# Loading the last chunk of the wq weights as 112 rows and two times 8 rows, so that half of the DMA engines carry more of it

## Chip, cores, metric

One core of one Trainium2 chip. The metric is the device time of one execution in microseconds (us), lower is better; the span of a profiled execution is about 2 us shorter than its device time (138.2 against 140.57 us before the change).

## The reference, cut to what matters

A decode step of one transformer block for 4 sequences: layer norm, attention with 32 query heads over the last 2048 cached positions, then a gated feed-forward layer.

```python
# x [4,1,1024]; caches [4,4,8192,128]; wq [1024,4096]; wo [4096,1024]; w1,w3 [1024,3584]; w2 [3584,1024]
q = layernorm(x) @ wq                       # the first use of weights; wq is the first tensor loaded
p = softmax(q @ k^T * Dh**-0.5)             # k, v: the last 2048 positions
h = x + (p @ v) @ wo
out = h + (silu(ln(h) @ w1) * (ln(h) @ w3)) @ w2      # ln: layernorm
```

There are only 4 rows of activations, so nearly all the work is reading 55.6 MB of weights and cache once.

## The kernel before

Everything large goes through one ten-deep pool of tiles of 128 partitions x up to 16 KB in SBUF, the core's on-chip memory. The Sync engine issues the loads in a fixed order (wq, k, v, wo, w1, w3, w2), as far ahead as the pool allows. A wq chunk puts two neighbouring rows of the weights on each partition: one run of 16 KB of HBM per partition. "Rows" below are partitions of such a tile.

```python
stream = ctx.enter_context(tc.tile_pool(name="stream", bufs=10))
wq_v = A_wq.rearrange("(p kc) n -> p kc n", kc=KC)       # KC = 8, KPC = 2: four chunks

def load_wq(c):
    wq_t = stream.tile([P, KPC, Hq * Dh], BF16, tag="s")
    nc.sync.dma_start(out=wq_t[:], in_=wq_v[:, c * KPC : (c + 1) * KPC, :])
    return wq_t

plan = (
    [("wq", load_wq, (c,)) for c in range(KC // KPC)]
    + [("k", load_k, (b,)) for b in range(B)]
    # ... v, wo, w1, w3
    + [("w2", load_w2, (j, [4, 3] if j < JG - 1 else [3, 2, 1, 1])) for j in range(JG)]
)
# ... load_next(10) at the start; one more whenever a tile has been used
```

Of the kernel before, what the change touches and what calls it, by code (L numbers as in the profile page):

```python
# [10 lines left out]
P = 128  # L11
# [8 lines left out]
def kernel(  # L20
# [13 lines left out]
    nc = tc.nc  # L34
# [7 lines left out]
    KC = D // P  # L42
# [36 lines left out]
    KPC = 2  # L79
# [3 lines left out]
    wq_v = A_wq.rearrange("(p kc) n -> p kc n", kc=KC)  # L83
# [2 lines left out]

    def load_wq(c):
        wq_t = stream.tile([P, KPC, Hq * Dh], BF16, tag="s")
        nc.sync.dma_start(out=wq_t[:], in_=wq_v[:, c * KPC : (c + 1) * KPC, :])
        return wq_t  # L90

    def load_k(b):
# [33 lines left out]
    def load_w2(j, pieces):  # L126
# [6 lines left out]
# [4 lines that stand above are left out]
        + [("v", load_v, (b,)) for b in range(B)]  # L137
# [26 lines left out]
    for j in range(JG):  # L164
        nc.scalar.dma_start(
            out=x_q[QD * j : QD * j + B, :], in_=x_flat[:, j * CG : (j + 1) * CG]
# [7 lines left out]
    for c in range(2):  # L174
# [8 lines left out]
        out=xn[:], in0=x_sb[:], scalar1=mv[:, 0:1], scalar2=rstd[:, 0:1],  # L183
# [25 lines left out]
    for j in range(2, JG):  # L209
        nc.vector.tensor_tensor(  # L210
            out=same[:, 0, :], in0=same[:, 0, :], in1=ident[:, j * QD : (j + 1) * QD], op=ALU.add
# [6 lines left out]
    for kc in range(KC):  # L218
        wq_t = loaded["wq"][kc // KPC]
# [16 lines left out]
    for r in range(REP):  # L236
        nc.tensor.transpose(out=qt_ps[:, r, :], in_=q_sb[:, r * Dh : (r + 1) * Dh], identity=ident[:])
    nc.vector.tensor_copy(
        out=qz[:, :, : Hkv * QD].rearrange("p b (g z) -> p b g z", g=Hkv)[:, :, :, :REP],
        in_=qt_ps[:].rearrange("p r (g x) -> p x g r", g=Hkv)[:, :B, :, :],  # L240
# [24 lines left out]
    for u, (b, n) in enumerate(units):  # L265
        k_v = loaded["k"][b][:].rearrange("p (j d) -> p j d", d=Dh)
        kT = ktpool.tile([P, NJ, P], BF16, tag="kT")
        for t in range(NJ // TB):
            kt_ps = psA.tile([P, TB, P], BF16, tag=f"kt{nt % 4}")
            for jj in range(TB):  # L270
                nc.tensor.transpose(  # L271
                    out=kt_ps[:, jj, :], in_=k_v[:, n * NJ + t * TB + jj, :], identity=ident[:]
# [23 lines left out]
        out=Pm[:].rearrange("q (c jq) -> q jq c", jq=NSB), in_=scores_ps[:].rearrange("q (jq c) -> q jq c", jq=NSB),  # L296
# [42 lines left out]
    for hh in range(RPO):  # L339
        nc.vector.tensor_copy(  # L340
            out=o4[hh * MP : (hh + 1) * MP, :, :, :].rearrange("p h r b -> p r h b"),
            in_=o4_ps[hh * MP : (hh + 1) * MP, :, :, hh, :],
# [12 lines left out]
    for h4 in range(Hq // RPO):  # L355
# [35 lines left out]
        out=hn[:], in0=h1[:], scalar1=tot[:, 0:1], scalar2=rstd2[:, 0:1],  # L391
# [5 lines left out]
    for r in range(KPC):  # L397
# [3 lines left out]
        out=hnT[:], in_=hn_ps[:].rearrange("p r (j x) -> p j r x", j=JG)[:, :, :, :B]  # L401
# [34 lines left out]
    for i in range(IF):  # L436
# [3 lines left out]
        out=hgT[:], in_=hg_ps[:].rearrange("p i (j x) -> p i j x", j=JG)[:, :, :, :B]  # L440
# [52 lines left out]
```

## Time and profile before

| | before |
|---|---|
| time, median | 140.01 us (3 runs), 140.41 us over 6 runs |
| span of the profiled execution | 138.2 us |
| moved by DMA | 55.74 MB |
| PE (TensorE matmuls) busy | 54% of the span |

The DMA engines bound it. On the page, the two rows of the second part that matter are the mean busy share of the core's 16 DMA engines (in tenths, 40 slices of 3.5 us) and what they moved:

```profile
span 138.2 us, 2365 instructions
...
DMA  5999999999999999999999999999999999999950
GB/s 154 433 423 436 417 436 436 441 413 432 441 402 409 420 421 416 425 423 430 429 429 417 425 442 424 428 432 428 432 428 432 432 432 413 421 427 430 409 216 2
```

Between the first slice and the last two there is no dip: time is bytes over rate, and what lowers the rate anywhere is paid at the end. The chain of work that ended last says the same; its PE part runs beside a queue that stays full (DMA share 1.01 from 35 to 128 us).

```profile
DMA 74%; PE 16%; ACT 5%; SPq 1%; issue 1%; DVE 0%; ACTq 0%
```

The table by stretches (start:end, length, then busy us and instructions of PE, of PE's weight loads, of VectorE, ScalarE and GpSimd, then the granted clock, the DMA share and GB/s) gives the rate. The last wq chunk is loaded from about 17 to 22 us, then comes k:

```profile
12.00:17.00 5.00, 1.88 (x16) 0.51 (x16) 0.00 (x0) 0.00 (x0) 0.00 (x0) 1.00 0.99 423
17.00:23.00 6.00, 2.23 (x20) 0.61 (x23) 0.00 (x0) 0.00 (x0) 0.00 (x0) 1.00 1.01 434
23.00:29.00 6.00, 4.23 (x39) 2.46 (x32) 1.40 (x3) 0.60 (x1) 0.00 (x0) 1.00 1.02 437
29.00:35.00 6.00, 5.70 (x64) 4.07 (x63) 2.35 (x4) 3.79 (x4) 0.00 (x0) 1.00 1.00 426
```

And the same table shows the end, where the DMA share falls in steps because the engines do not end together:

```profile
130.00:132.00 2.00, 0.94 (x16) 0.45 (x19) 0.00 (x0) 0.00 (x0) 0.00 (x0) 0.50 1.00 408
132.00:133.00 1.00, 0.66 (x12) 0.26 (x5) 0.00 (x0) 0.00 (x0) 0.00 (x0) 0.50 0.72 283
133.00:134.00 1.00, 0.89 (x12) 0.32 (x12) 0.00 (x0) 0.00 (x0) 0.00 (x0) 0.50 0.43 164
```

The trace also has a record of every DMA packet (start, duration, size, queue). It does not name the engine, but an engine's next packet starts 3 to 4 ns before its last one ends, so its packets can be followed by their phase (what is said below of single engines is read in this way). Per engine a 128-row wq chunk is 8 packets of 16 KB at 0.611 us, one every 0.607 us. Eight packets of 16 KB belong to the queue that the page calls instruction (0.88 to 0.97 us each); they are called instruction fetches here after its name. After each of them one further engine lands every later DMA about 1.4 us behind; one 8 KB packet of another queue at 58.9 us costs one more engine 0.83 us. At the end seven engines are done at 132.2 to 132.5 us, one at 133.3 and eight at 133.6 to 133.9.

### The profile page before, as it was taken

The numbers are of one execution on the slowest core, as the hardware profiler recorded it, in microseconds if no ns is written. First come the engines' busy times: TensorE is split into PE (matmuls) and PEld (weight loads), VectorE is DVE, ScalarE is ACT, GpSimd is POOL, SyncE is SP. The second block draws the span as 40 slices with busy tenths as digits, with TensorE's granted clock in tenths as the row PEclk, the third lists the DMA queues.
The fourth block names the chain that finished last, engine by engine and source line by source line (L and its number), as shares of the span: only waits on it lengthen the run. The fifth ranks groups of instructions, "written<-read, shape, count | busy, mean of one in ns | idle before, by whom it ended". The sixth has DMA issues, their size and how long they took to land.

```text
span 138.2 us, 2365 instructions
## 1 busy us (share of the span) xinstructions
PE 75.0 (54%) x1057; PEld 43.4 (31%) x1057; DVE 37.1 (27%) x71; ACT 29.4 (21%) x29; POOL 0.7 (1%) x6
## 2 busy tenths in 40 slices
PE   0152254499798989300795489383244432663560
PEld 0111011295656556000795356131011110231220
DVE  6610000244343434520500460600008930300000
ACT  1200000126464646279420000000051000000000
POOL 2000000000000000000000000000000000000000
PEclk9999999999999999955555556855555555555555
DMA  5999999999999999999999999999999999999950
GB/s 154 433 423 436 417 436 436 441 413 432 441 402 409 420 421 416 425 423 430 429 429 417 425 442 424 428 432 428 432 428 432 432 432 413 421 427 430 409 216 2
DMA packets 7025, 55.74 MB, mean 403 GB/s; under 512 B 580, under 2 KB 612, under 8 KB 3560
## 3 DMA queue, kind: packets, MB, share of 16 engines
q1 hardware_dynamic: 6960, 55.58, 95.7%
q8 instruction: 8, 0.13, 0.3%
q10 hardware_dynamic: 56, 0.02, 0.1%
q14 instruction: 1, 0.01, 0.0%
HBM read 55.59 MB, written 0.01 MB: 402 GB/s over the span
## 4 chain that ended last, share of the span: by engine, by line
DMA 74%; PE 16%; ACT 5%; SPq 1%; issue 1%; DVE 0%; ACTq 0%
DMA w_t<-in_B_w_dram 55%; DMA k_t<-in_A_k_cache_dram 14%; PE kt_ps L271 10%; DMA wq_t<-in_A_wq_dram 5%; ACT kT L277 5%; PE scores_ps L256 5%; SPq L118 1%; PE y_ps L448 0%; DVE res L458 0%; ACT res L459 0%; SPq L111 0%; ACTq L277 0%
## 5 line engine op out<-in xcount | busy, mean ns | idle before, releaser
L277 ACT COPY kT<-kt_ps 128x1024 bf16<-128x1024 bf16 x16 | 15.9, 1013 | 14.5 <-PE kt_ps L271 14.5
L271 PE MATMUL kt_ps<-ident,k_t 128*128 128x128 bf16 x256 | 18.0, 231 | 0.9 <-DMA k_t<-in_A_k_cache_dram 0.9
L271 PEld LDWEIGHTS <-k_t 128*128 128x128 bf16 x256 | 15.9, 104 | 6.1 <-issue 4.9
L275 DVE COPY kT<-kt_ps 128x1024 bf16<-128x1024 bf16 x16 | 11.1, 692 | 17.6 <-PE kt_ps L271 17.6
L223 PE MATMUL q_ps<-wq_t,xnT 128*4 128x512 bf16 x64 | 7.5, 620 | 11.2 <-DMA wq_t<-in_A_wq_dram 11.2
L414 PE MATMUL u_ps<-w_t,hnT 128*4 128x448 bf16 x64 | 6.7, 567 | 10.3 <-DMA w_t<-in_B_w_dram 10.3
L256 PE MATMUL scores_ps<-kT,qz 128*32 128x512 bf16 x64 | 9.9, 609 | 3.0 <-ACT kT L277 3.0
L414 PEld LDWEIGHTS <-hnT 128*4 128x4 bf16 x128 | 3.9, 109 | 24.0 <-issue 23.4
L448 PE MATMUL y_ps<-w_t,hgT 128*4 128x256 bf16 x112 | 7.5, 404 | 6.3 <-DMA w_t<-in_B_w_dram 6.0
L414 PE MATMUL g_ps<-w_t,hnT 128*4 128x448 bf16 x64 | 6.5, 570 | 5.0 <-DMA w_t<-in_B_w_dram 4.7
L323 PE MATMUL OT_ps<-PT_sb,v_t 128*128 128x8 bf16 x256 | 7.4, 168 | 1.7 <-issue 1.4
L323 PEld LDWEIGHTS <-v_t 128*128 128x128 bf16 x256 | 7.3, 104 | 1.9 <-issue 1.7
L359 PE MATMUL y_ps<-wo_t,o_954 128*4 128x256 bf16 x128 | 6.4, 391 | 1.7 <-DVE y_ps L349 1.7
L223 PEld LDWEIGHTS <-xnT 128*4 128x4 bf16 x64 | 2.0, 106 | 15.8 <-issue 15.5
L309 PE MATMUL pt_ps<-Dm,Pm 128*128 128x128 bf16 x16 | 1.9, 308 | 9.3 <-DVE Dm L302 9.3
L459 ACT CAST res<-y_ps 128x128 bf16<-128x128 f32 x1 | 0.3, 267 | 31.0 <-DVE res L458 31.0
L448 PEld LDWEIGHTS <-hgT 128*4 128x4 bf16 x112 | 3.5, 103 | 10.3 <-issue 8.4
L427 DVE RECIPROCAL eg<-eg 128x896 f32<-128x896 f32 x1 | 5.8, 5753 | 0.0
L359 PEld LDWEIGHTS <-o_954 128*4 128x4 bf16 x128 | 4.0, 119 | 4.1 <-DVE y_ps L349 2.0
L233 DVE TENSOR_SCALAR q_sb<-q_ps 128x512 bf16<-128x512 f32 x1 | 0.7, 693 | 16.9 <-PE q_ps L223 16.9
L234 ACT ACTIVATE q_sb<-q_ps 128x512 bf16<-128x512 f32 x1 | 0.6, 597 | 20.9 <-DVE q_sb L233 20.9
L295 ACT ACTIVATE Pm<-scores_ps,nmax 128x2048 bf16<-128x2048 f32 x1 | 4.8, 4784 | 0.0
(73 smaller groups left out, 40.7 us busy)
## 6 DMA issues: line engine op xcount, KB each, us to landing
w_t<-in_B_w_dram SPq DMA_DIRECT2D x8, 1792.0 KB, 33.2
wq_t<-in_A_wq_dram SPq DMA_DIRECT2D x4, 2048.0 KB, 11.6
k_t<-in_A_k_cache_dram SPq DMA_DIRECT2D x4, 2048.0 KB
v_t<-in_A_v_cache_dram SPq DMA_DIRECT2D x4, 2048.0 KB, 40.4
wo_t<-in_A_wo_dram SPq DMA_DIRECT2D x4, 2048.0 KB
w_t<-in_B_w_dram SPq DMA_DIRECT2D x3, 1024.0 KB
w_t<-in_B_w_dram SPq DMA_DIRECT2D x4, 768.0 KB, 29.7
w_t<-in_B_w_dram SPq DMA_DIRECT2D x1, 512.0 KB
```

What stands on the lines that cost most here:

```text
L223: nc.tensor.matmul(q_ps[QD * g : QD * g + B, hf * 512 : (hf + 1) * 512], lhsT=xnT[:, kc, :], rhs=wq_t[:, kc % KPC, c0 : c0 + 512], start=( ...
L256: nc.tensor.matmul(scores_ps[QD * g : QD * (g + 1), n * 512 : (n + 1) * 512], lhsT=qz[:, b, g * QD : (g + 1) * QD], rhs=kT_v[:, g, :, :], ...
L271: nc.tensor.transpose(out=kt_ps[:, jj, :], in_=k_v[:, n * NJ + t * TB + jj, :], identity=ident[:])
L275: nc.vector.tensor_copy(out=kT[:, t * TB : (t + 1) * TB, :], in_=kt_ps[:])
L277: nc.scalar.copy(out=kT[:, t * TB : (t + 1) * TB, :], in_=kt_ps[:])
L295: nc.scalar.activation(out=Pm[:].rearrange("q (c jq) -> q jq c", jq=NSB), in_=scores_ps[:].rearrange("q (jq c) -> q jq c", jq=NSB), func=A ...
L309: nc.tensor.matmul(pt_ps[:, jj, :], lhsT=Pm[:, (jb * JPB + jj) * P : (jb * JPB + jj + 1) * P], rhs=Dm[:], start=True, stop=True)
L323: nc.tensor.matmul(OT_ps[:, b, g * REP : (g + 1) * REP], lhsT=v_t[:, g, j, :], rhs=PT_sb[:, j, g * QD + b * REP : g * QD + (b + 1) * REP], ...
L359: nc.tensor.matmul(y_ps[QD * j : QD * j + B, :], lhsT=o4[:, h4, r, :], rhs=wo_t[:, h4 % (HPC // RPO), r, j * CG : (j + 1) * CG], start=(h4 ...
L414: nc.tensor.matmul(out_ps[QD * j : QD * j + B, hf, :HF], lhsT=hnT[:, k2, r, :], rhs=w_t[:, r, c0 : c0 + HF], start=(k2 == 0 and r == 0), s ...
L427: nc.vector.reciprocal(out=eg[:], in_=eg[:])
L448: nc.tensor.matmul(y2_ps[QD * j : QD * j + B, :], lhsT=hgT[:, i, jf, :], rhs=w2_t[:, i, j * CG : (j + 1) * CG], start=False, stop=(jf == J ...
```

## The change

Its intent is to even out that end. The last wq chunk is cut into 112 rows, which all 16 engines load (7 rows each), and twice 8 rows, which only eight of them load. Those eight carry 9 packets of this chunk and the other eight carry 7. The trace of the changed kernel shows it: the 112-row DMA has 16 landings, and each of the sixteen engines has 7 packets of it; the two 8-row DMAs have 8 landings each; and when the next load, the first k tile, has landed, eight engines lie within 0.66 us of the first and eight 1.22 to 1.83 us behind it.

```diff
     def load_wq(c):
         wq_t = stream.tile([P, KPC, Hq * Dh], BF16, tag="s")
-        nc.sync.dma_start(out=wq_t[:], in_=wq_v[:, c * KPC : (c + 1) * KPC, :])
+
+        cuts = [0, P] if c < KC // KPC - 1 else [0, P - 16, P - 8, P]
+        for p0, p1 in zip(cuts[:-1], cuts[1:]):
+            nc.sync.dma_start(out=wq_t[p0:p1], in_=wq_v[p0:p1, c * KPC : (c + 1) * KPC, :])
         return wq_t
```

## The prediction

> **What bounds the kernel.** The DMA engines. The page gives a span of 138.2 us, 55.74 MB at 403 GB/s, a DMA share of 9 tenths or more in nearly every slice, PE 54% busy. In the chain of waits DMA has 74%; its last piece is the last of w2 (landed at 134.29 us), then about 0.8 us of matmuls and copies. The PE stretch in that chain (27.5 to 57 us) costs nothing: the queue stays full beside it, and a load issued at 58.4 us lands 33 us later.
>
> **The tail is uneven.** In the table by stretches the DMA share is 1.00 up to 132 us, then 0.72 and 0.43. The trace's packet records show why. Each engine moves one 16 KB wq row in 0.607 us, back to back. Eight 16 KB instruction fetches (0.88 to 0.97 us each) each put one further engine about 1.4 us behind for good; an 8 KB packet at 58.9 us puts another 0.83 us behind. So seven engines end at 132.2 to 132.5 us, one at 133.3, eight at 133.6 to 133.9. Followed by phase, the four engines that load x took none of the eight fetches; one of them took the 8 KB packet. [...] I infer that the late eight are the upper half.
>
> **What the change does.** [...] Lower half: 9 packets for the chunk instead of 8; upper half 7: +0.607 us and -0.607 us. SP issues two more DMAs (0.33 to 0.42 us each), early, under a full queue: nothing. The last wq chunk lands later: off the path.
>
> **Case A: rows cost what they cost now.** Upper half ends at 133.0 to 133.3, seven lower engines at about 133.1, but the one with the 8 KB packet at 133.3 + 0.6 = 133.9, where the end is today. Gain 0 to 0.1 us, at most 0.6: 139.4 to 140.2 us.
>
> **Case B: the destination is narrow.** Rows 112 to 119, then 120 to 127, are written by eight engines at once. [...] all of it on the critical path: 143 to 145 us. No run so far shows such a limit: every large load has 128 rows.
>
> I hold B slightly likelier (55%).
>
> **Predicted:** 142.0 us, 8 times in 10 within 139.6 to 145.2. Faster by over 2%: 0.01; within 2%: 0.46; slower: 0.53.
>
> **What would show it.** Packets of the two small DMAs: 0.61 us means A, 2 us or more B. The tail: in B a DMA share near 0.5 for 3 us or more; in A all engines end within about 1 us. wq's last chunk lands 0.6 us later in A, 4 or more in B.
>
> **What would make it wrong.** The late engines being the lower half (A then costs 0.6 us); the 112-row DMA colliding on ports too (worse than B); the semaphore rotation, shifted by two DMAs, draining the queue.

"Lower half" and "lower engines" are the eight engines that load the 8 rows, "upper half" the other eight; "port" is a way into SBUF that rows share, an assumption that no trace names. Case B came to 143 to 145 us, which is 3.6 to 4.8 us over the 139.4 to 140.2 of case A; it stands as the author's estimate.

## The result

| | before | after |
|---|---|---|
| time, median of 6 runs | 140.41 us | 146.96 us |
| ratio to before | 1 | 1.0474, 95% interval 1.0449 to 1.0499 |
| span of the profiled execution | 138.2 us | 144.9 us |

A ratio here is the mean time of one kernel's fast runs over the mean of the other's fast runs of the same rounds, so it is not quite the ratio of the medians. Executions over 1.5% slower than the fastest of the same kernel are left out of the means. The measured time lies above the predicted range (139.6 to 145.2). Which step of the prediction failed is told below.

The page after, the lines that answer to those of before:

```profile
span 144.9 us, 2368 instructions
...
DMA  5999999799999999999999999999999999999940
GB/s 156 426 435 434 425 280 213 100 407 434 425 430 417 399 420 421 421 417 427 430 425 430 423 425 437 424 439 427 427 424 427 439 431 413 425 424 426 413 187 2
...
DMA 74%; PE 15%; ACT 5%; SPq 2%; issue 1%; DVE 0%; ACTq 0%
```

Read the two rows together. For three slices the bytes moved fall to 280, 213 and 100 GB/s, while the share of busy DMA engines stays at 9 tenths or more in two of them. It reads 7 in the third, because a packet is counted whole in the slice in which it starts; the stretches below give 1.03 there. The engines are not idle; their packets take longer. All other slices before the end are much as before. The stretches:

```profile
12.00:17.00 5.00, 1.88 (x16) 0.51 (x16) 0.00 (x0) 0.00 (x0) 0.00 (x0) 1.00 0.98 419
17.00:23.00 6.00, 1.88 (x16) 0.38 (x15) 0.00 (x0) 0.00 (x0) 0.00 (x0) 1.00 1.03 306
23.00:29.00 6.00, 0.00 (x0) 0.00 (x0) 0.00 (x0) 0.00 (x0) 0.00 (x0) 1.00 1.03 134
29.00:35.00 6.00, 3.47 (x28) 1.48 (x29) 0.98 (x2) 0.60 (x1) 0.00 (x0) 1.00 0.99 418
```

Between 17 and 29 us the kernel moves 6 x 306 + 6 x 134 = 2640 KB where before it moved 6 x 434 + 6 x 437 = 5226 KB. The missing 2.59 MB, at 425 GB/s, are 6.1 us of the 6.7 us of longer span. Most of the rest is a less even end, the opposite of the intent: in the last 5 us before the last packet of w2 ends, the packet records leave each engine idle for 0.75 us on average before the change and for 1.16 us after it. Nothing is given back later, and the end is moved:

```profile
136.00:138.00 2.00, 0.81 (x12) 0.37 (x12) 0.00 (x0) 0.00 (x0) 0.00 (x0) 0.50 0.99 407
138.00:139.00 1.00, 0.51 (x12) 0.36 (x12) 0.00 (x0) 0.00 (x0) 0.00 (x0) 0.50 0.90 352
139.00:140.00 1.00, 0.56 (x16) 0.20 (x9) 0.00 (x0) 0.00 (x0) 0.00 (x0) 0.50 0.42 162
140.00:141.00 1.00, 0.72 (x12) 0.13 (x5) 0.00 (x0) 0.00 (x0) 0.00 (x0) 0.50 0.09 33
```

The fourth group of matmuls on wq shows the late chunk, here from the timeline of PE, before and after:

```profile
22.65 1.88 PE L223 MATMUL q_ps<-wq_t,xnT 128*4 128x512 bf16 x16 [3.02 <-DMA wq_t<-in_A_wq_dram]
```

```profile
30.30 1.88 PE L226 MATMUL q_ps<-wq_t,xnT 128*4 128x512 bf16 x16 [10.34 <-DMA wq_t<-in_A_wq_dram]
```

The packet records give two separate losses:

- The 112-row DMA. It starts at 17.1 to 17.5 us and its sixteen engines are through at 23.0 to 23.7 us: about 6.0 us for 7 packets that need 7 x 0.607 = 4.25 us. In the middle of it a packet takes 0.91 us on average instead of 0.61.
- The two 8-row DMAs. From 23.5 to 29.6 us 29 packets take more than 2 us, 2.37 us on average. They are not only those of the eight engines that load the 8 rows, which have 16 packets there in all. The other eight, already on the first k tile, are slowed by as much. Between 23 and 29 us, 6 x (437 - 134) = 1818 KB are missing, 4.3 us at 425 GB/s.

### The profile page after: what moved, and what is told of

The parts are those of the page before. It is cut to its first block, busy times and chain, and to the rows that moved or that the text cites. A ratio compares the mean times of both kernels' runs of the same rounds, so it can differ in the third digit from the quotient of the medians.

```text
span 144.9 us, 2368 instructions
## 1 busy us (share of the span) xinstructions
PE 75.1 (52%) x1057; PEld 43.4 (30%) x1057; DVE 37.1 (26%) x71; ACT 29.4 (20%) x29; POOL 0.7 (0%) x6
## 4 chain that ended last, share of the span: by engine, by line
DMA 74%; PE 15%; ACT 5%; SPq 2%; issue 1%; DVE 0%; ACTq 0%
DMA w_t<-in_B_w_dram 51%; DMA k_t<-in_A_k_cache_dram 18%; PE kt_ps L274 10%; DMA wq_t<-in_A_wq_dram 5%; ACT kT L280 5%; PE scores_ps L259 5%; SPq L121 2%; SPq L92 0%; SPq L114 0%; PE y_ps L451 0%; DVE res L461 0%; ACT res L462 0%; ACTq L280 0%
## 5 line engine op out<-in xcount | busy, mean ns | idle before, releaser
L278 DVE COPY kT<-kt_ps 128x1024 bf16<-128x1024 bf16 x16 | 11.1, 692 | 17.1 <-PE kt_ps L274 17.1
```

The lines of the kernel that those rows point to most:

```text
L278: nc.vector.tensor_copy(out=kT[:, t * TB : (t + 1) * TB, :], in_=kt_ps[:])
```

## Experiments

The theories at the start: **P**, rows of SBUF that lie close together share a way in (a port) and its rate; **S**, reading neighbouring rows of the weights from HBM at once is slow; **H**, DMAs on half the engines, or row counts other than 128, are slow as such. Time differences in us are (ratio - 1) x 140.4.

### Where the rows are read or where they are written?

Three kernels, each the kernel before with two extra loads of 8 rows x 8 KB behind the last wq chunk, into a tile that nobody reads. They differ only in the rows. The line that makes the pool `scr` is left out here. "Lower eight" is used for the eight engines that load such 8 rows, "upper eight" for the others.

```diff
+    scr_t = scr.tile([P, Hq * Dh], BF16)
     ...
-    load_next(10)
+    load_next(4)
+    for d, r in PAIRS:
+        nc.sync.dma_start(out=scr_t[d], in_=wq_v[r, 6, :])
+    load_next(6)
# d_packed:      d = 112:120 and 120:128;     r = 112:120 and 120:128
# d_spread_dst:  d = 0:32:4 and 32:64:4;      r = 112:120 and 120:128
# d_spread_src:  d = 112:120 and 120:128;     r = 0:128:16 and 8:128:16
```

> The kernel before, with two extra loads of 8 rows x 8 KB on the lower eight engines behind the last wq chunk, into a scratch tile, rows 112 to 119 and 120 to 127, from the same wq rows. A normal 8 KB packet takes 0.309 us. Theory P (destination rows share few SBUF ports): these 16 packets take 1.2 us or more and the time rises by 2 to 3.5 us. Theory S (adjacent source rows in HBM collide): the same. Theory H (any DMA on half the engines is slow, or the second slowdown comes from the odd count of rows): H-half the same; if only the 112-row DMA was at fault, packets 0.31 us and at most +0.1 us.

> As d_packed, the same source rows, but written to rows 0,4,..,28 and 32,36,..,60[...]. Theory P: packets 0.31 us, time +0 to +0.3 us. Theory S and theory H-half: packets 1.2 us or more, +2 to 3.5 us as d_packed.

> As d_packed, destination rows 112 to 119 and 120 to 127, but read from wq rows 0,16,..,112 and 8,24,..,120. Theory P: as d_packed, +2 to 3.5 us. Theory S: packets 0.31 us, +0 to +0.3 us. Theory H-half: as d_packed.

The 1.2 us is what the changed kernel's slow packet gives when it is scaled to 8 KB: 2.37 x 0.309 / 0.611.

| run | ratio (95%) | difference | the sixteen 8 KB packets | 16 KB packets over 0.7 us, 16 to 32 us |
|---|---|---|---|---|
| d_packed | 1.0125 (1.0106 to 1.0143) | +1.8 us | up to 1.09 us | 26, mean 1.35 us |
| d_spread_dst | 1.0031 (1.0008 to 1.0054) | +0.4 us | all 0.309 us | none |
| d_spread_src | 1.0134 (1.0110 to 1.0157) | +1.9 us | up to 1.00 us | 31, mean 1.25 us |

The rate from 22 to 25 us, in d_packed:

```profile
22.00:25.00 3.00, 1.42 (x16) 0.38 (x15) 0.00 (x0) 0.00 (x0) 0.00 (x0) 1.00 0.98 216
```

in d_spread_dst:

```profile
22.00:25.00 3.00, 1.88 (x16) 0.38 (x15) 0.31 (x1) 0.00 (x0) 0.00 (x0) 1.00 1.01 429
```

and in d_spread_src:

```profile
22.00:25.00 3.00, 1.18 (x12) 0.38 (x15) 0.00 (x0) 0.00 (x0) 0.00 (x0) 1.00 1.02 216
```

Spreading the destination takes all slow packets away (the two loads are 131 KB, 0.3 us at 425 GB/s, of the +0.4 us that stay); spreading the source takes none of the loss away. DMAs of the same bytes, also on eight engines, run at full speed (0.309 us a packet) when the rows they write lie four apart. S falls, and so does the part of H that blamed DMAs on eight engines. In size the expectation was somewhat high (+2 to 3.5 us), and not all 8 KB packets were slow: on most engines the first of the two is recorded at 0.309 us, and the waiting shows on the packets behind it.

In the trace of d_spread_dst the four engines that load x are all among the eight with the extra packets.

### Does the loss need half the engines or an odd row count?

The last wq chunk in two DMAs of 64 rows, all engines in both (DMA share 0.99 and 1.01 in the stretches below); once as two contiguous halves, once as even and odd rows.

```diff
# c_64_64, against the kernel after
-        cuts = [0, P] if c < KC // KPC - 1 else [0, P - 16, P - 8, P]
+        cuts = [0, P] if c < KC // KPC - 1 else [0, P // 2, P]
# c_even_odd, against the kernel before
-        nc.sync.dma_start(out=wq_t[:], in_=wq_v[:, c * KPC : (c + 1) * KPC, :])
+        step = 1 if c < KC // KPC - 1 else 2
+        for p0 in range(step):
+            nc.sync.dma_start(out=wq_t[p0:P:step], in_=wq_v[p0:P:step, c * KPC : (c + 1) * KPC, :])
```

> The last wq chunk as two DMAs of 64 rows, all sixteen engines in both, no engine left out. Theory P (ports): [...] the chunk takes twice its 4.86 us, packets of about 1.2 us: +4.9 us, +3.5%. A theory by which only DMAs on eight engines, or odd row counts such as 112, are slow: packets 0.61 us, +0 to +0.1 us.

> The last wq chunk as two DMAs of 64 rows again, but of every second row[...]. Theory P alone with engines kept apart on the ports: no loss, +0 to +0.2 us, against +5.3 us of the two contiguous halves. Theory P with a DMA's rows dealt to the engines in runs (engine e gets the e-th sixteenth of the rows), which fits the 112 rows: [...] packets of about 1.1 us and +4 us. Theory N (it is the number of rows, 64 instead of 128, not the ports): +5 us as the contiguous halves.

The factor of two of c_64_64 and the 1.1 us of c_even_odd were estimates; no run had shown their grounds.

c_64_64: ratio 1.0383 (1.0365 to 1.0401), +5.4 us; 145 slow packets with a mean of 1.205 us, twice the normal 0.611. c_even_odd: ratio 0.9997 (0.9970 to 1.0024); every packet 0.611 us. The stretch from 22 to 25 us of c_64_64, then of c_even_odd:

```profile
22.00:25.00 3.00, 0.00 (x0) 0.00 (x0) 0.00 (x0) 0.00 (x0) 0.00 (x0) 1.00 0.99 208
```

```profile
22.00:25.00 3.00, 1.88 (x16) 0.38 (x16) 0.49 (x1) 0.00 (x0) 0.00 (x0) 1.00 1.01 431
```

With two contiguous halves the rate is half: 208 against 431 GB/s. With even and odd rows the same number of rows, DMAs and bytes costs nothing. So for 64 rows it is neither their count nor the number of DMAs. One expectation for c_even_odd (+4 us, from rows dealt to the engines in runs) was refuted. How rows are placed on engines in a partial DMA is therefore not what I had assumed, and stays open.

### The 112 rows by themselves

```diff
# extra load into the unused tile, as above, one DMA
# d_112:  d = 0:112, r = 0:112        d_128:  d = 0:128, r = 0:128
```

> The kernel before with one extra load of 112 rows x 8 KB into a scratch tile: 7 packets of 0.309 us per engine, 2.16 us if they do not collide. In the changed kernel the 112-row DMA took about 6.0 us for 7 packets that need 4.25, a factor of 1.4. If that is a property of the 112-row shape [...]: about 3.1 us, +2.2%. If it came from the 8-row DMAs waiting behind it: 2.16 us, +1.5%.

> Control for the extra load of 112 rows, which cost 3.4 us: the same with all 128 rows. 8 packets of 0.309 us on every engine: 2.47 us without collisions (packets 0.31 us), so less time for more bytes. If any extra load of 1 MB costs more than its packets, over 3.4 us.

The stretch from 22 to 25 us of d_112, then of d_128:

```profile
22.00:25.00 3.00, 1.88 (x16) 0.38 (x15) 0.00 (x0) 0.00 (x0) 0.00 (x0) 1.00 1.21 380
```

```profile
22.00:25.00 3.00, 1.88 (x16) 0.38 (x15) 0.17 (x1) 0.00 (x0) 0.00 (x0) 1.00 1.03 437
```

d_112: ratio 1.0245 (1.0218 to 1.0272), +3.4 us; median packet 0.406 us, up to 0.67. d_128: ratio 1.0172 (1.0148 to 1.0196), +2.4 us; every packet 0.309 us. Loading 112 rows costs more than loading 128: 3.4 us for what would be 7 x 0.309 = 2.16 us. The 112-row shape is slow with no 8-row DMA near it, as the first of the two expectations had it. Why it is slow stays open: the trace does not name rows, and the expectation's reason assumed the way of dealing rows to engines that c_even_odd refuted.

### One DMA of 16 rows in place of two of 8

```diff
# c_112_16, against the kernel after
-        cuts = [0, P] if c < KC // KPC - 1 else [0, P - 16, P - 8, P]
+        cuts = [0, P] if c < KC // KPC - 1 else [0, P - 16, P]
```

> The change with the last 16 rows as one DMA [...] instead of two of 8. The 112-row DMA should cost what it does in the changed kernel (packets of about 0.9 us in place of 0.61, +1.7 us). Theory P: the 16 rows[...] take about 2.4 us a packet: +1.8 us more, about +3.5 us in all. Theory H-half (only DMAs on eight engines are slow) and the 112 rows alone: 0.61 us a packet, +1.7 us in all. Theory S: between.

Ratio 1.0304 (1.0284 to 1.0324), +4.3 us, against +6.7 us of the change. The 112-row part is as slow as in the change (300 and 306 GB/s between 17 and 23 us):

```profile
17.00:23.00 6.00, 1.88 (x16) 0.38 (x15) 0.00 (x0) 0.00 (x0) 0.00 (x0) 1.00 1.07 300
```

The difference of 2.4 us is about one slow packet of the change (mean 2.37 us): the same 256 KB are one DMA here, and two behind each other in the change. The expectation of theory P, an estimate, was +3.5 us, too low by 0.8. Its packets of 2.4 us did not come either: the longest took 2.08 us, and the 25 over 1.4 us took 1.69 us on average.

### Why do the engines that do not take part slow down?

```diff
# as d_packed;  d_low_packed, d_low_packed2:  d = 0:8 and 8:16
```

> As d_packed, but the two extra loads write rows 0 to 7 and 8 to 15. Two theories for why in d_packed and in the changed kernel the other eight engines slowed too, though they were already on the next 128-row load. Theory B [...]: all sixteen engines slow as in d_packed, time +1.2% (140.4 to 142.2). Theory O (only engines that write to the same ports wait): [...] the engines that do not take part keep 0.61 us a packet and the loss falls on the lower eight alone, +0.3 to +1.3%.

> The extra loads into rows 0 to 7 and 8 to 15 again, because its profiled execution was a disturbed one of 189 us. Theory B [...]: between 22 and 25 us about 26 to 31 packets of 16 KB at 0.7 to 1.9 us, most of them on engines without the extra loads, as in the packed loads to rows 112 to 127. Theory O: 16 KB packets of the engines without extra loads stay at 0.61 us.

Theory B is that the crowded rows hold up all sixteen engines, theory O that they hold up only the engines that write there.

Ratio of the first 1.0106 (1.0089 to 1.0123), of the second 1.0114 (1.0080 to 1.0148). The time could not tell the two theories apart; the ranges I had written overlap. The packets can, and because the first one's profile was a disturbed execution of 189 us, they are read from the second: 32 packets of 16 KB over 0.7 us between 16 and 32 us, mean 1.06 us. Followed by phase, every engine has at least one of them, most of the engines without extra packets two. Its stretch:

```profile
22.00:25.00 3.00, 1.47 (x16) 0.38 (x15) 0.00 (x0) 0.00 (x0) 0.00 (x0) 1.00 1.06 292
```

The packets of the engines without extra loads did not stay at 0.61 us, as theory O had it: 8-row loads into rows 0 to 15 hold up all sixteen engines (292 GB/s in this stretch), as those into rows 112 to 127 did in the change (134 GB/s from 23 to 29 us). So a few crowded rows seem to slow the whole core's loads, not only those to these rows. The trace does not name rows: the reading takes it that most of the k packets were headed for other ones. What the loads share, no run tells.

### Was the intent sound?

Two runs. d_spread4 adds four 8-row loads into rows four apart (0.309 us a packet in d_spread_dst), so that the lower eight engines (those that such DMAs use) carry 4 x 0.309 = 1.24 us more. c_intent is the change's split, 9 packets against 7, built from strided rows.

```diff
# d_spread4:  d = 0:32:4, 32:64:4, 1:32:4, 33:64:4;  r = 112:120, 120:128, 96:104, 104:112
# c_intent, the last chunk of wq:
+        rows = [slice(0, P)]
+        if c == KC // KPC - 1:
+            rows = [slice(1, P, 4), slice(2, P, 4), slice(3, P, 4), slice(64, P, 4), slice(0, 32, 4), slice(32, 64, 4)]
+        for s in rows:
+            nc.sync.dma_start(out=wq_t[s], in_=wq_v[s, c * KPC : (c + 1) * KPC, :])
```

> As d_spread_dst with four such loads: the lower eight engines carry 4 x 0.309 = 1.24 us more, without collisions. In d_spread_dst three or more of the eight instruction fetches seemed to fall on the lower eight. Theory M (fetches fall on both halves): the end moves by about the whole 1.24 us, +0.9%. Theory U (all late engines are the upper half, as the prediction inferred): the lower engines end at 133.7, with the 8 KB packet 134.5: +0.6 us, +0.4%.

> The change's intent with as few collisions as possible: the last wq chunk in strided DMAs, three of 32 rows and one of 16 (rows 64,68,..,124) on all engines and two of 8 (rows 0,4,..,28 and 32,36,..,60) on the lower eight, so again 9 packets for each lower engine and 7 for each upper one. Theory P: only the 16 rows collide[...]; the 8-row packets take 0.61 us. The prediction's case A (the late eight are the upper half) then gives +0.5 to +0.7 us. If fetches fall on both halves, a late lower engine gets 0.61 us on top: +1.0 to +1.3 us, +0.7 to +0.9%. In neither is it faster than before.

In c_intent's sums the totals (+0.5 to +0.7 and +1.0 to +1.3 us) stand as estimates.

d_spread4: ratio 1.0050 (1.0030 to 1.0070), +0.7 us: between the two expectations (+0.4% and +0.9%). The spans of its four runs were 138.9 to 139.4 us, against 138.0 to 138.2 us before. Its trace settles more, because the extra load separates the halves. When the first k tile lands, eight engines are within 0.52 us of the first and eight are 1.20 to 1.67 us behind it. Each instruction fetch can then be given to a half by which of these drops back: the first two fetches (32.6 and 43.7 us) hit engines of the lower half, the next ones the upper half. In d_spread_dst it was the third, fourth and eighth (53.9, 73.4 and 127.9 us) that hit the lower half. In both the 8 KB packet did too. The traces of the changed kernel and of c_intent mark the halves too, and show the same: two of the eight fetches and the 8 KB packet on the lower half (38.5 and 49.5 us in the changed kernel, 80.5 and 87.0 us in c_intent). So most fetches fall on the upper half, but not all, and not the same ones in each of these four traces. Giving the lower eight more to carry then delays engines of which some are late already.

c_intent: ratio 1.0081 (1.0035 to 1.0128), +1.1 us, and its only slow packets are 27 around the 16-row DMA (mean 0.91 us). It agrees with the expectation for fetches on both halves (+0.7 to 0.9%); its interval also holds the other (+0.5 to 0.7 us), so as a time it is inconclusive. Its trace is clearer: the 27 packets cost 27 x (0.91 - 0.61) / 16 = 0.5 us per engine, and the idle time at the end, taken as above, is 1.23 us per engine against 0.75 before. So with most of the slow packets gone the split makes the end less even, and is not faster. No version here beats the kernel before.

## Why the prediction was wrong

- **What bounds the kernel: right.** The DMA engines, at a rate that no other stage limits (425 GB/s from 35 to 128 us, before and after). The lost bytes reappear in the time (6.1 of the 6.7 us).
- **Case B: right in kind.** Packets of 2 us or more were its sign, and there are 29, mean 2.37. The last wq chunk lands late, as B said (its matmuls begin at 30.30 us, not at 22.65). Where the rows are written, and not where they are read, decides (429 GB/s in d_spread_dst against 216 in d_spread_src). What makes neighbouring rows slow, no run shows.
- **The step that failed is "+0.607 us and -0.607 us"**, that is, counting the 112-row DMA at 7 packets of 0.607 us. It took about 6.0 us instead of 4.25: its packets took 0.91 us in the middle of it. d_112 shows that the 112 rows are slow without the change's other DMAs, and c_112_16 that they are slow beside one of 16 rows; why is not shown. The prediction named it under "what would make it wrong" but put no number on it. Adding the measured 1.8 us to case B (143 to 145 us) gives 144.8 to 146.8; the time of 146.96 lies just above that.
- **Case B's 3.6 to 4.8 us over case A: the size was near, the place was wrong.** The terms that are cut put the loss on the lower eight. It holds up all sixteen: the other half's k packets took as long, and the loss is 4.3 us of bytes not moved between 23 and 29 us. So the sign that the prediction gave for B in the tail, a DMA share near 0.5 for 3 us or more, did not come (0.90, 0.42 and 0.09 in the last three stretches of 1 us).
- **The stated centre, 142.0 us, belonged to neither case**; it was a middle between 140 and 144. Nearly half the weight lay on case A, for which no run gave support.
- **"The late eight are the upper half": wrong as a rule.** In the four traces where the halves can be told apart, two or three of the eight fetches fell on the lower half. For the kernel before itself it stays open, since its trace does not mark the halves. So case A's estimate was too kind as well: the end became less even by 0.4 us per engine (0.75 to 1.16), where it was to become more even. The three parts, 1.8 + 4.3 + 0.4, make 6.5 of the 6.7 us.
- **The semaphore rotation draining the queue, named as a risk: not seen.** In the trace the landings of successive loads come on eight semaphores in turn, and the Sync engine waited longer for loads of wq to land before it issued others (21.1 us in total, before 6.8). But the DMA share from 23 to 29 us is 1.03 while the rate is 134 GB/s.

## What to carry to other kernels

When a load is cut by partitions, ask which rows of SBUF each piece writes: in this kernel, bound by DMA, the pieces of 8, 16 and 64 neighbouring rows ran slowly (134 GB/s from 23 to 29 us in the change, 175 from 23 to 26 us in c_112_16, 208 from 22 to 25 us in c_64_64), and those of 8 held up the other loads of the core for as long as they lasted. The 112 rows were slow too, for a reason that is not shown. Pieces that cost nothing here were all 128 rows of some columns (as w2 is loaded, at 424 GB/s between 120 and 130 us), every second row (ratio 0.9997), and every fourth of all 128 rows (no slow packet in c_intent); every fourth row of the upper 64 alone did cost time (c_intent's 16-row DMA, 27 packets with a mean of 0.91 us). Before shifting work between engines, check in more than one trace that the late ones are the same ones each time.
